# Making a part of the softmax exponentials as sums of fp16 bit patterns, with TensorE adding them up and GpSimd making one of them

## Chip, cores, metric

The kernel runs on one core of a Trainium2 chip. The metric is the device time of one execution in microseconds (us). Each kernel was run several times beside runs of the kernel before on the same chip. A run counts as "slow" when it is over 1.5% above the fastest run of the same kernel.

## The reference, cut to what matters

Two attention problems (32 heads of 16, 2048 positions) stand side by side. "A" works on four segments with a mask and a memory term. "B" is plain attention over all 2048 keys, and is most of the work:

```python
scores = jnp.einsum('bhqd,bhkd->bhqk', q, k) * Dh ** (-0.5)
p = _softmax(scores, axis=-1)
o = jnp.einsum('bhqk,bhkd->bhqd', p, v)
```

B has 4 query chunks x 4 row tiles x 2 = 32 units. A unit has 16 key blocks, and a key block has four banks of 128 keys x 512 queries (four heads), so 64 banks a unit. Each bank needs one exp of 128x512.

## The kernel before

ScalarE makes most of the exps, straight from PSUM, in tiles of alternately three and two banks. VectorE makes the exps of two of 16 key blocks of each unit but the first, by a polynomial on the bits of an fp16 number. TensorE makes scores (four 32-row matmuls can share the array), the products with V ("PV": four 32-column matmuls share it), the projections ("chores"), and fillers: matmuls on zeros, added into a live accumulator, whose only use is to keep TensorE's clock up. The order on each engine is fixed when the program is built.

```python
PESHARE = 0.74          # share of a tile's time that TensorE is to be filled to
VSHARE = 1.0            # dose of VectorE work a tile
VQUADS = 2              # key blocks of 16 that VectorE makes
PBUFS = 6
... # cut
        def idle_work(us):
            work[0] = min(max(work[0] - us * PESHARE, -1.0), 0.25)
            acc = accs.get(cur[0])
            while acc is not None and work[0] < -0.11:
                mm(acc[:], zeros[:, 0:P], zeros[:], start=False, stop=False, skip_group_check=True)
... # cut
        def vexp(q, xq):                 # xq: scores of one key block, scaled, as uint16 (128 x 2048)
            ... # cut
            ts(f[:].bitcast(U16), xq[:], 0x3FF, 0x3C00, ALU.bitwise_and, ALU.bitwise_or)
            tt(v[:], f[:], f[:], ALU.mult)
            ts(v[:], v[:], C3, C1 - 1.0, ALU.mult, ALU.add)
            tt(v[:], v[:], f[:], ALU.mult)
            ts(v[:], v[:], C0, 1024.0, ALU.add, ALU.mult)
            tt(xq[:].bitcast(I16), xq[:], v[:], ALU.add)
            ... # cut: handed to PV as one block
... # cut
        for t in range(NT):              # one tile of 3 or 2 banks
            run_until(t)
            scores(t)                    # TensorE scores, ScalarE exp
            did = pv(t - LAG, 2)         # up to two ready blocks
            ... # cut: chores
            idle_work(0.1 + 0.427 * len(tiles[t][0]))
            flush()
            vscores(t)                   # one bank of scores for VectorE, evicted as scaled uint16
            vfill(...)                   # pieces of VectorE work, as far as their dose goes
```

Scores for VectorE, PV accumulators and projections share three PSUM banks (`misc`). The ScalarE tiles have the other five.

## Time and profile before

| | before |
|---|---|
| time, median | 1050.2 us (of three runs; of the four of the result below, 1050.0) |
| ScalarE (ACT) busy | 984.7 of 1055.6 us |
| exps on ScalarE | 848 tiles, 973.5 us |
| filler matmuls | 1053 |
| mean granted TensorE clock | 0.976 |
| time at half clock | 52 us |

The first part of the page, busy time by engine:

```profile
span 1055.6 us, 17191 instructions
PE 967.6 (92%) x6822; PEld 277.2 (26%) x6822; DVE 759.8 (72%) x1108; ACT 984.7 (93%) x877; POOL 169.9 (16%) x335
```

Its second part, rows of 40 equal slices: busy tenths of PE and ACT, and the granted clock in tenths.

```profile
PE   8899999998999989999998999999999999999996
...
ACT  3799999998999989999999899999999999999995
...
PEclk8999999998999989999999899999999999999998
```

ACT is busy nearly throughout, apart from the start and the end. PE looks as busy, but a third of its matmuls' busy time are fillers, as the groups show (columns: line, engine, operation, out<-in, forms, count | busy us, mean ns | idle before, and what ended it):

```profile
L655 ACT ACTIVATE pT<-s_ps 128x1536 bf16<-128x1536 f32 x848 | 973.5, 1314 | 57.7 <-PE s_ps L80 53.0
...
L80 PE MATMUL acc<-zeros 128*128 128x512 bf16 x1053 | 321.6, 390 | 0.0
...
L596 DVE TENSOR_SCALAR vv<-vv 128x2048 f16<-128x2048 f16 x124 | 86.7, 699 | 2.2
L599 DVE TENSOR_TENSOR vv<-vf 128x2048 f16<-128x2048 f16 x62 | 76.2, 1229 | 1.9
```

The page also follows the chain of work that ended last back from the end, and gives each engine's share of it. ACT has the largest:

```profile
ACT 40%; PE 31%; issue 12%; DVE 11%; POOL 3%; DMA 1%; SPq 0%; ACTq 0%; DVEq 0%; POOLq 0%
```

The timeline at 299 us shows VectorE and GpSimd getting in each other's way (start, length, engine, what):

```profile
299.40 2.69 POOL L186 TENSOR_SCALAR qA<-qc,par 128x512 bf16<-128x512 bf16 x2 [18.40 <-DVE qc L183]
...
299.94 1.59 DVE L599 TENSOR_TENSOR vx<-vx,vv 128x2048 int16<-128x2048 uint16 x1
```

The VectorE operation takes 1.59 us instead of its usual 1.22, and the two GpSimd operations together 2.69 instead of about 1.4.

The waits: what ScalarE loses to TensorE, and what TensorE loses to VectorE's exps (total us, times, longest us).

```profile
ACT pT L655 <- PE s_ps L80: 53.0, 61, 8.0
...
PE acc L80 <- DVE vx L599: 3.9, 7, 1.0
...
PE v_ps L80 <- DVE vx L689: 0.7, 2, 0.5
```

### The profile page before, as it was taken

Reading aid. Unit: us, or ns where it says so; the run is one execution under the profiler, and the core shown is the slowest. Engines: PE = TensorE matmul, PEld = TensorE weight load, DVE = VectorE, ACT = ScalarE, POOL = GpSimd, SP = SyncE. Lnnn points to the kernel's source line nnn. Section 1 sums busy time; section 2 is a strip of 40 time slices with the busy share of each in tenths; the row PEclk is TensorE's granted clock in tenths of the full one; section 3 lists DMA queues with packets and bytes.
Section 4 is the critical chain, followed back from the end, with each engine's and each line's share of the span. In section 5 each row is a group of like instructions: output and inputs, shape, how many; then the busy total and the mean of one; then the engine's idle time right before and its main releaser. Section 6 shows DMA issues by size and latency. Waiting matters only on the chain.

```text
span 1055.6 us, 17191 instructions
## 1 busy us (share of the span) xinstructions
PE 967.6 (92%) x6822; PEld 277.2 (26%) x6822; DVE 759.8 (72%) x1108; ACT 984.7 (93%) x877; POOL 169.9 (16%) x335
## 2 busy tenths in 40 slices
PE   8899999998999989999998999999999999999996
PEld 2222222222222222222222222222222222222221
DVE  2668787866888677788876788858576787776654
ACT  3799999998999989999999899999999999999995
POOL 3721210403013030030302204021020300000000
PEclk8999999998999989999999899999999999999998
DMA  8400000001000000010000000000000000000000
GB/s 179 100 7 21 6 2 6 1 2 25 6 1 13 29 7 6 2 25 6 2 6 1 21 26 1 7 1 1 2 1 1 2 30 11 1 1 2 1 1 25
DMA packets 35642, 15.36 MB, mean 15 GB/s; under 512 B 27360, under 2 KB 35552, under 8 KB 35552
## 3 DMA queue, kind: packets, MB, share of 16 engines
q1 hardware_dynamic: 33776, 13.78, 5.5%
q8 instruction: 55, 0.90, 0.4%
q10 hardware_dynamic: 1776, 0.40, 0.2%
q14 instruction: 35, 0.29, 0.1%
HBM read 4.20 MB, written 4.19 MB: 8 GB/s over the span
## 4 chain that ended last, share of the span: by engine, by line
ACT 40%; PE 31%; issue 12%; DVE 11%; POOL 3%; DMA 1%; SPq 0%; ACTq 0%; DVEq 0%; POOLq 0%
ACT pT L655 39%; PE acc L80 14%; PE s_ps L80 8%; PE v_ps L80 5%; DVE vv L599 2%; DVE vx L689 2%; POOL pT L663 2%; PE q_ps L80 1%; PE k_ps L80 1%; DVE vx L599 1%; PE o_ps L80 1%; DVE vv L596 1%; ACT ex L194 1%; DVE vf L596 1%; DVE tT L253 1%
## 5 line engine op out<-in xcount | busy, mean ns | idle before, releaser
L655 ACT ACTIVATE pT<-s_ps 128x1536 bf16<-128x1536 f32 x848 | 973.5, 1314 | 57.7 <-PE s_ps L80 53.0
L80 PE MATMUL s_ps<-qB,KB 32*128 32x512 bf16 x1800 | 310.8, 384 | 35.0 <-ACT pT L655 30.5
L80 PE MATMUL acc<-zeros 128*128 128x512 bf16 x1053 | 321.6, 390 | 0.0
L689 DVE TENSOR_SCALAR vx<-v_ps 128x512 uint16<-128x512 f32 x248 | 169.1, 683 | 122.2 <-PE v_ps L80 65.7
L80 PEld LDWEIGHTS <-KB 32*128 32x128 bf16 x2048 | 99.6, 91 | 339.6 <-issue 326.7
L663 POOL TENSOR_SCALAR_AFFINE_SELECT pT<-pT 128x256 bf16<-128x256 bf16 (+2 forms) x242 | 111.0, 487 | 322.7 <-ACT pT L655 322.1
L80 PE MATMUL acc<-pT,VB 128*32 128x512 bf16 x1800 | 144.4, 385 | 1.2 <-DVE tT L253 1.2
L80 PEld LDWEIGHTS <-zeros 128*128 128x128 bf16 x1069 | 84.6, 99 | 147.2 <-issue 111.7
L253 DVE STREAM_TRANSPOSE tT<-acc 128x512 f32<-128x512 f32 x64 | 45.7, 714 | 94.1 <-PE acc L80 93.9
L80 PE MATMUL v_ps<-qB,KB 32*128 32x512 bf16 x248 | 95.5, 385 | 9.2 <-DVE aT L260 3.4
L596 DVE TENSOR_SCALAR vv<-vv 128x2048 f16<-128x2048 f16 x124 | 86.7, 699 | 2.2
L599 DVE TENSOR_TENSOR vv<-vf 128x2048 f16<-128x2048 f16 x62 | 76.2, 1229 | 1.9
L599 DVE TENSOR_TENSOR vx<-vx,vv 128x2048 int16<-128x2048 uint16 x62 | 76.0, 1226 | 1.2
L599 DVE TENSOR_TENSOR vv<-vv,vf 128x2048 f16<-128x2048 f16 x62 | 76.0, 1227 | 1.1
L80 PE MATMUL s_ps<-qA,kA 32*128 32x384 bf16 (+3 forms) x512 | 56.8, 313 | 9.9 <-ACT pT L655 7.8
L186 POOL TENSOR_SCALAR qB<-qc,par 128x512 bf16<-128x512 bf16 x32 | 26.0, 823 | 232.1 <-DVE qc L183 229.2
L80 PEld LDWEIGHTS <-VB 128*32 128x32 bf16 x2048 | 32.4, 94 | 73.9 <-issue 73.8
L596 DVE TENSOR_SCALAR vf<-vx 128x2048 uint16<-128x2048 uint16 x62 | 43.3, 699 | 1.5
L186 POOL TENSOR_SCALAR qA<-qc,par 128x512 bf16<-128x512 bf16 x32 | 25.7, 815 | 114.9 <-DVE qc L183 114.8
L80 PE MATMUL acc<-pT,vA 128*32 128x128 bf16 (+3 forms) x512 | 39.0, 332 | 5.6 <-POOL pT L663 3.2
L80 PEld LDWEIGHTS <-kA 32*128 32x128 bf16 x512 | 17.8, 92 | 63.1 <-issue 61.2
L80 PE MATMUL acc<-vx,VB 128*32 128x512 f16 x248 | 24.7, 386 | 4.6 <-DVE vx L599 3.9
(88 smaller groups left out, 510.8 us busy)
## 6 DMA issues: line engine op xcount, KB each, us to landing
out_dram<-osb SPq DMA_DIRECT2D x31, 128.0 KB, 1.7
w_b<-in_B_wqkv_dram SPq DMA_DIRECT2D x3, 512.0 KB, 6.0
phk<-phkT SPq DMA_TRANSPOSE x48, 2.3
w_a<-in_A_wv_dram SPq DMA_DIRECT2D x1, 512.0 KB, 7.0
wo_a<-in_A_wo_dram SPq DMA_DIRECT2D x1, 512.0 KB, 4.1
wo_b<-in_B_wo_dram SPq DMA_DIRECT2D x1, 512.0 KB, 5.0
w_a<-in_A_wk_dram SPq DMA_DIRECT2D x1, 384.0 KB, 7.5
w_a<-in_A_wq_dram SPq DMA_DIRECT2D x1, 384.0 KB, 8.2
```

What stands on the lines that cost most here:

```text
L80: return pin(nc.tensor.matmul(out, lhsT, rhs, **k))
L186: pin(nc.gpsimd.tensor_scalar(dst[:, e, :], qc[:], par[:, e:e + 1], 0.0, ALU.mult, ALU.add))
L194: pin(nc.scalar.activation(ex[:], src, ACT.Exp))
L253: vlater(0.72, lambda: pin(nc.vector.transpose(st["tT"][:, e].rearrange("p c d -> p (c d)"), acc)))
L596: pin(nc.vector.tensor_scalar(o, i, s1, s2, op0, op1))
L599: pin(nc.vector.tensor_tensor(o, i0, i1, op=op))
L655: pin(nc.scalar.activation(pT[:, 0:n, :], pt[:, 0:n, :], ACT.Exp, scale=SCALE))
L663: pin(nc.gpsimd.affine_select(out=blk, in_=blk, compare_op=ALU.is_ge, fill=0.0, base=0, pattern=[[0, len(sls)], [1, P]], channel_multiplie ...
L689: pin(nc.vector.tensor_scalar(x[0][:, vb[0], :], vt[:], XSCALE, 15360.0, ALU.mult, ALU.add))
```

## The change

The intent: take more exps off the bounding ScalarE. An fp16 bit pattern `x + offset` is a piecewise linear approximation of 2^x. Five such patterns at different offsets add up to a good exp, and the adding is free for VectorE, because TensorE sums them in PV. VectorE then needs four cheap adds a block instead of six operations, and one of the four is given to GpSimd. So VectorE can serve four and three key blocks of alternate units instead of two. A new `force()` makes sure that buffers are free: if the probabilities of six tiles ago are not yet used, it issues pending PV and VectorE pieces at once.

```diff
-C0, C1, C3 = 0.4580543, 0.4656991, 0.0762947
+LADDER = (12521, 12721, 12834, 13081, 13329)
-VQUADS = 2
+VBUFS = 9
+VQUADS = (4, 3)
+VPOOL = 1
...
-        def vexp(q, xq):            (six operations, shown above)
+        def vexp(q, buf, x):
+            for i, off in enumerate(LADDER[1:]):
+                yield 0.0 if i < VPOOL else 0.70
+                f = vtile()
+                if i < VPOOL:
+                    pin(nc.gpsimd.tensor_scalar(f[:], x[:], 1.0, float(off - LADDER[0]), ALU.mult, ALU.add))
+                else:
+                    pin(nc.vector.tensor_scalar(f[:], x[:], float(off - LADDER[0]), 32767.0, ALU.add, ALU.min))
+                vready(q, [1], f, 2 * (i < VPOOL))      # each pattern is one more PV block
+                vdone(buf)
...
         def scores(t):
+            while apend.get(t - PBUFS):
+                force()
...
+        def force():
+            if pv(NT, 1):
+                return
+            if vwork and vlive[0] < VBUFS:
+                vpiece(vwork)
+                return
+            assert step_chore()
... (cut: the plan of which tile gets which bank, separate weight tiles to free memory, bounds of the sums)
```

More of the change, by code (lines that the diff above doesn't have):

```diff
@@ L31 @@
 MASK_NEG = -1.0e9
-SUMS = {"a": (2.0 ** -8, 2.0 ** 31), "b": (2.0 ** 7, 2.0 ** 15.5)}
+SUMS = {"a": (2.0 ** -8, 2.0 ** 31), "b": (2.0 ** 9, 2.0 ** 15)}
 XSCALE = SCALE * 1.4426950408889634 * 1024
-C0, C1, C3 = 0.4580543, 0.4656991, 0.0762947
+LADDER = (12521, 12721, 12834, 13081, 13329)
 PESHARE = 0.74
@@ L41 @@
 VSHARE = 1.0
-VWAIT = 3
-VQUADS = 2
+VBUFS = 9
+VQUADS = (4, 3)
+VEND = 0.83
+VLEAD = 12
+VPOOL = 1
 BANKS = (3, 2)
@@ L135, in masks_gates, with load_w @@
         pin(nc.vector.scalar_tensor_tensor(grow[:], gv[:, :, 1], par[:, 1:2], grow[:], ALU.mult, ALU.add))
-    def load_w(pool, name):
-        t = pool.tile([P, 4, 3 * D], BF16, name=f"w_{name}", tag=f"w_{name}")
+    def load_w(homes, name):
+        t = [p.tile([P, 4, D], BF16, name=f"w_{name}", tag=tag, bufs=bufs) for p, tag, bufs in homes]
         srcs = ([B_wqkv[:, i * D:(i + 1) * D] for i in range(3)] if name == "b" else [A_wq, A_wk, A_wv])
         def load(eng, i, lo=0, hi=D):
-            eng.dma_start(out=t[:, :, i * D + lo:i * D + hi],
+            eng.dma_start(out=t[i][:, :, lo:hi],
                           in_=srcs[i][:, lo:hi].rearrange("(cc p) n -> p cc n", p=P))
@@ L169, in do_k @@
         for cc in range(4):
-            mm(ps[:], w[:, cc, D + rt * P:D + (rt + 1) * P], xT[:, cc, :], start=(cc == 0), stop=(cc == 3))
+            mm(ps[:], w[1][:, cc, rt * P:(rt + 1) * P], xT[:, cc, :], start=(cc == 0), stop=(cc == 3))
             if cc == 3:
@@ L178, in do_q @@
         for cc in range(4):
-            mm(ps[:], w[:, cc, rt * P:(rt + 1) * P], xT[:, cc, :], start=(cc == 0), stop=(cc == 3))
+            mm(ps[:], w[0][:, cc, rt * P:(rt + 1) * P], xT[:, cc, :], start=(cc == 0), stop=(cc == 3))
             if cc < 3:
@@ L204, in do_v @@
         for cc in range(4):
-            mm(ps[:], xT[:, cc, kb * P:(kb + 1) * P], w[:, cc, 2 * D:3 * D], start=(cc == 0), stop=(cc == 3))
+            mm(ps[:], xT[:, cc, kb * P:(kb + 1) * P], w[2][:, cc, :], start=(cc == 0), stop=(cc == 3))
             if cc == 3:
@@ L335 @@
         mp = ps_a = ms.enter_context(tc.tile_pool(name="ps_a", bufs=3, space=PSUM))
-        wA, ld = load_w(big, "a")
+        wA, ld = load_w([(big, f"wa{i}", 1) for i in range(3)], "a")
         ld(nc.scalar, 1, 0, P)
@@ L345 @@
         ld(nc.sync, 0, P)
-        wB, ld = load_w(big, "b")
+        wB, ld = load_w([(big, "wb0", 1)] + [(wk, "vx", VBUFS)] * 2, "b")
         ld(nc.sync, 1)
@@ L391 @@
                         quads_left[u["id"]] = quads_left.get(u["id"], 0) + 1
-                spans.append([(name, ch, rt), banks, []])
+                spans.append([(name, ch, rt), banks, None])
             else:
                 for u in us:
-                    quads_left[u["id"]] = S // P
-                    nv = VQUADS if nb else 0
-                    if nb:
-                        spans[-1][2].extend((u, kb) for kb in range(nv))
+                    nv = u["nv"] = VQUADS[nb % 2] if nb else 0
+                    quads_left[u["id"]] = S // P + nv * (len(LADDER) - 1)
@@ L400 @@
                     spans.append([(name, ch, rt) if u is u0 else None,
-                                  [(j, [(u, kb, 0, 512, 0)]) for kb in range(nv, S // P) for j in q4], []])
+                                  [(j, [(u, kb, 0, 512, 0)]) for kb in range(nv, S // P) for j in q4], u])
                     nb += 1
-        for i in range(1, len(spans)):
-            key = spans[i][0]
-            if key and key[0] == "a" and spans[i][2]:
-                spans[i - 1][1] += spans[i][1]
-                spans[i - 1][2] += spans[i][2]
-                spans[i - 1].append((key, len(spans[i - 1][1]) - len(spans[i][1])))
-                spans[i] = None
@@ L411 @@
-        first_tile, tiles = {}, []
-        vq = deque()
-        act = deque()
-        def close(n, v=None):
-            tiles.append(([act.popleft() for _ in range(n)], v))
-        for sp in spans:
-            if sp is None:
-                continue
-            starts = {0: sp[0]} if sp[0] else {}
-            for key, at in sp[3:]:
-                starts[at] = key
-            for u, kb in sp[2]:
-                vq.append((u, kb, set(q4)))
-            nv, na, placed = sum(len(left) for *_, left in vq), len(sp[1]), 0
-            for i, bank in enumerate(sp[1]):
-                if i in starts:
-                    first_tile[starts[i]] = len(tiles)
-                act.append(bank)
-                n = BANKS[len(tiles) % 2]
-                if len(act) < n:
-                    continue
-                v = None
-                if vq and placed < nv and (placed + 0.5) * na <= nv * (i + 1):
-                    js = vq[0][2] - {j for j, _ in act}
-                    if js:
-                        j = min(js)
-                        u, kb, left = vq[0]
-                        left.discard(j)
-                        if not left:
-                            vq.popleft()
-                        first_tile.setdefault(("v", u["ch"], u["rt"]), len(tiles))
-                        v = (j, (u, kb, 0, 512, 0))
-                        placed += 1
-                close(n, v)
@@ L446 @@
-        assert not vq
-        while act:
-            close(min(BANKS[len(tiles) % 2], len(act)))
+        first_tile, tiles, act, tile_of = {}, [], deque(), []
+        for key, banks, u in spans:
+            if key:
+                first_tile[key] = len(tiles)
+            if u:
+                u["lo"] = len(tile_of)
+            for bank in banks:
+                act.append(bank)
+                tile_of.append(len(tiles))
+                if len(act) == BANKS[len(tiles) % 2]:
+                    tiles.append([act.popleft() for _ in range(len(act))])
+            if u:
+                u["hi"] = len(tile_of)
@@ new lines, with plan @@
+        while act:
+            tiles.append([act.popleft() for _ in range(min(BANKS[len(tiles) % 2], len(act)))])
+        vplan = deque()
+        bs = [u for *_, u in spans if u]
+        def plan(u, kbs, lo, hi):
+            for i in range(4 * len(kbs)):
+                t = tile_of[int(lo - VLEAD + (i + 0.5) * (hi - lo) / (4 * len(kbs)))]
+                first_tile.setdefault(("v", u["ch"], u["rt"]), t)
+                vplan.append((t, u, kbs[i // 4]))
+        for u, nxt in zip(bs, bs[1:] + [None]):
+            n = max(u["nv"], 2)
+            cut = u["lo"] + (u["hi"] - u["lo"]) * ((n - 1) / n if nxt and nxt["lo"] == u["hi"] else VEND)
+            plan(u, range(1, u["nv"]), u["lo"], cut)
+            if nxt:
+                plan(nxt, range(1), cut, nxt["lo"])
@@ L520, in b_kv_chores, with counted @@
             v_ones(VB, S // P)
+            left = {"k": S // P, "v": S // P}
+            def counted(which, g):
+                yield from g
+                left[which] -= 1
+                vlive[0] -= left[which] == 0
             for rt in range(NRT):
@@ L524, in b_kv_chores @@
                     chore(min(d, first_tile.get(("v", 0, rt), NT)) if ch == 0 else d,
-                          do_k(mp, wB, xTB[ch], rt, KB[:, rt, ch * W:(ch + 1) * W]))
+                          counted("k", do_k(mp, wB, xTB[ch], rt, KB[:, rt, ch * W:(ch + 1) * W])))
             for sb in range(S // P):
                 chore(first_tile[("b", 0, 0)] + 4 + 4 * sb // 3,
-                      do_v(mp, wB, xTB[sb // 4], sb % 4, v_heads(VB, sb)[:, :, 0:DH]))
-        vfin, vwork, credit = deque(), deque(), [0.0]
+                      counted("v", do_v(mp, wB, xTB[sb // 4], sb % 4, v_heads(VB, sb)[:, :, 0:DH])))
+        vfin, vwork, credit, vlive = deque(), deque(), [0.0], [2]
         held[0] = []
@@ L577 @@
         last_s, cur = [None], [0]
-        pvq = []
+        pvq, forced = [], [0]
         accs, OT = {}, {}
@@ L589, in score, with vready, vdone, vtile @@
             mm(dst[:, col:col + w], k, q, start=first, stop=True, tile_position=(32 * j, 0), skip_group_check=True)
-        vx, live = {}, [0]
-        def vexp(q, xq):
-            def ts(o, i, s1, s2, op0, op1):
-                pin(nc.vector.tensor_scalar(o, i, s1, s2, op0, op1))
-            def tt(o, i0, i1, op):
-                pin(nc.vector.tensor_tensor(o, i0, i1, op=op))
-            yield 0.69
-            assert live[0] < 3
-            live[0] += 1
-            f = wk.tile([P, 4, 512], F16, name="vf", tag="vf")
-            v = wk.tile([P, 4, 512], F16, name="vv", tag="vv")
-            ts(f[:].bitcast(U16), xq[:], 0x3FF, 0x3C00, ALU.bitwise_and, ALU.bitwise_or)
-            yield 1.22
-            tt(v[:], f[:], f[:], ALU.mult)
-            yield 0.69
-            ts(v[:], v[:], C3, C1 - 1.0, ALU.mult, ALU.add)
-            yield 1.22
-            tt(v[:], v[:], f[:], ALU.mult)
-            yield 0.69
-            ts(v[:], v[:], C0, 1024.0, ALU.add, ALU.mult)
-            yield 1.22
-            tt(xq[:].bitcast(I16), xq[:], v[:], ALU.add)
-            pd = xq[:].bitcast(F16)
+        vx, apend = {}, {}
+        def vready(q, buf, x, late=0):
             u, kb = q
-            pvq.append(dict(u=u, kb=kb, t=now[0], v=True, parts=[(pd, j, j, (u, kb, 0, 512, 0)) for j in q4]))
+            pd = x[:].bitcast(F16)
+            pvq.append(dict(u=u, kb=kb, t=now[0] + late, v=buf, parts=[(pd, j, j, (u, kb, 0, 512, 0), None) for j in q4]))
             pvq.sort(key=lambda q: q["u"]["id"])
+        def vdone(buf):
+            buf[0] -= 1
+            vlive[0] -= buf[0] == 0
+        def vtile():
+            assert vlive[0] < VBUFS
+            vlive[0] += 1
+            return wk.tile([P, 4, 512], U16, name="vx", tag="vx", bufs=VBUFS)
+        def vexp(q, buf, x):
[8 more added lines that the diff above has]
+                vdone(buf)
         def vpiece(wq):
@@ L635, in vfill @@
                 wq = vfin or vwork
-                if wq is vwork and live[0] == 3 and not wq[0][2]:
+                if wq is vwork and vlive[0] == VBUFS:
                     return
@@ L646, in scores @@
         def scores(t):
-            banks, vb = tiles[t]
+            banks = tiles[t]
+            while apend.get(t - PBUFS):
+                force()
             pt = last_s[0] = ps_s.tile([P, BANKS[t % 2], 512], F32, name="s_ps", tag=f"s{t % 2}")
@@ L671, in scores @@
                         pvq.append(q)
-                    q["parts"].append((pT, sl, j, seg))
+                    q["parts"].append((pT, sl, j, seg, t))
                     q["t"] = t
+                    apend[t] = apend.get(t, 0) + 1
             pvq.sort(key=lambda q: q["u"]["id"])
         def vscores(t):
-            vb = tiles[t][1]
-            if vb is None:
-                return
-            vt = mp.tile([P, 512], F32, name="v_ps", tag="misc")
-            score(vt[:], vb[0], vb[1], True)
-            u, kb = vb[1][0:2]
-            if (u["id"], kb) not in vx:
-                while len(vwork) >= VWAIT:
-                    vpiece(vwork)
-                vx[u["id"], kb] = [wk.tile([P, 4, 512], U16, name="vx", tag="vx", bufs=VWAIT + 2), 0]
-            x = vx[u["id"], kb]
-            pin(nc.vector.tensor_scalar(x[0][:, vb[0], :], vt[:], XSCALE, 15360.0, ALU.mult, ALU.add))
-            x[1] += 1
-            if x[1] == 4:
-                vpush(vwork, vexp((u, kb), x[0]))
+            n = 0
+            while vplan and vplan[0][0] <= t and n < 1 + (vplan[0][0] < t - 3):
+                _, u, kb = vplan[0]
+                if (u["id"], kb) not in vx:
+                    if vlive[0] > VBUFS - 2:
+                        break
+                    vx[u["id"], kb] = [vtile(), set(q4)]
+                vplan.popleft()
+                x, left = vx[u["id"], kb]
+                j = min(left, key=lambda j: (j in {j for j, _ in tiles[t]}, j))
+                left.discard(j)
+                vt = mp.tile([P, 512], F32, name="v_ps", tag="misc")
+                score(vt[:], j, (u, kb, 0, 512, 0), True)
+                pin(nc.vector.tensor_scalar(x[:, j, :], vt[:], XSCALE, float(LADDER[0]), ALU.mult, ALU.add))
+                n += 1
+                if not left:
+                    buf = [len(LADDER)]
+                    vready((u, kb), buf, x)
+                    vpush(vwork, vexp((u, kb), buf, x))
+            return n
+        def force():
+            forced[0] += 1
+            if pv(NT, 1):
+                return
+            if vwork and vlive[0] < VBUFS:
+                vpiece(vwork)
+                return
+            assert step_chore()
         def unit_done(u):
@@ L739, in pv @@
                 pvq.remove(q)
-                live[0] -= "v" in q
+                if "v" in q:
+                    vdone(q["v"])
                 if u["id"] not in accs:
@@ L746, in pv @@
                 v = vA[u["ch"]] if u["name"] == "a" else VB
-                for pT, sl, j, (_, kb, col, w, c0) in q["parts"]:
+                for pT, sl, j, (_, kb, col, w, c0), at in q["parts"]:
+                    if at is not None:
+                        apend[at] -= 1
                     h = 8 * u["rt"] + 2 * j + u["e"]
@@ L770 @@
                 step_chore()
-            idle_work(0.1 + 0.427 * len(tiles[t][0]))
+            idle_work(0.1 + 0.427 * len(tiles[t]))
             flush()
-            vscores(t)
-            vfill((0.08 + 0.427 * len(tiles[t][0])) * VSHARE - (0.69 if tiles[t][1] else 0.0))
+            vfill((0.08 + 0.427 * len(tiles[t])) * VSHARE - 0.69 * vscores(t))
             flush()
@@ L779 @@
         flush()
-        vdrain(vwork)
+        assert not vplan
+        while vwork:
+            force()
         ot = OT[("b", NSEG - 1)]
@@ L841, in exact_problem @@
                 nc.gpsimd.memset(neg[32 * j:32 * j + 1, :], -1.0)
-            w, ld = load_w(big, name)
+            w, ld = load_w([(big, f"w{i}", 1) for i in range(3)], name)
             for i in (1, 0, 2):
```

## The prediction

> **What bounds the kernel now.** ScalarE. The page's first part gives ACT 984.7 of 1055.6 us, of which the exps `pT<-s_ps` are 973.5. By form: 424 tiles of three banks and 424 of two, so 0.459 us a bank of 512 columns. ACT idles 71 us: 24 in the first 50 us (busy by stretches), 53 behind PE's `s_ps` in all (the waits). PE shows 968 us busy, but 1053 of its matmuls are fillers on `zeros`, 0.216 us start to start in the timeline: 227 us. DVE 760 us (72%), POOL 170.
>
> **What the change does** (counted in the instruction order of both builds).
> - ACT: key blocks of B given to VectorE go from 62 to 108 (four banks each), s_ps banks of B from 1800 to 1616. ACT loses 184 x 0.459 = 84.5 us.
> - DVE: the polynomial goes: per block 3 x 0.70 + 3 x 1.23 = 5.8 us, x62 = 358 us. In come 184 more evictions `vx<-v_ps` (0.683), 126 us, and 324 adds on 128x2048, which I cost like `vf<-vx` (0.699), 226 us. DVE stays at about 755 us, in 7% less time.
> - PE: PV of VectorE blocks goes from 248 to 2160 matmuls. Four share the array (0.216 us a group; a change between row, column and full tiling costs 0.1 more, timeline), so +1728 net is +93 us. Fillers fall from 1053 to 387 (-144 us). My sum of groups and changes is 810 us after, 867 before: no new bound, though early stretches reach 93% of ACT's time.
> - POOL: 108 adds on 128x2048. `qA` and `qB` ops (512 columns) take 0.69 us undisturbed, masking shows 0.89 ns a column over 0.18 us; I estimate 2.2 us each, 240 us, POOL about 400.
>
> **The catch** is the shared port. The Trainium skill, "SBUF — State Buffer", section "Who interferes with whom", says that VectorE in a two-port mode, or with two SBUF inputs, and GpSimd lock each other out for a whole instruction. The trace agrees: at 300 us a `vx<-vx,vv` between two `qA` ops took 1.59 us instead of 1.22, the second `qA` 1.65 instead of 0.69. So far POOL's ops are short. The new one holds 2.2 us, and DVE's adds stand right after it. PSUM evictions don't collide. With a third of DVE's ops colliding, I estimate 1 us of DVE blocked per POOL add, some 110 us. Then DVE needs about 865 of 950 us; in the middle, where demand already is 54 of each 60 us of ACT, more than ACT's time. Late evictions hold the three `misc` banks, PE waits in order, scores come late, ACT idles.
>
> **On the critical path.** ACT's 84 us are nearly all on it (exp is 39% of the chain of waits; the rest mostly feeds it). I expect 15 to 25 us given back as ACT idle behind `s_ps`: 1050 - 84 + 19 = 985 us, range 950 to 1022. Faster by over 2%: 0.89; within 2%: 0.08; slower: 0.03.
>
> **What would show it.** `pT<-s_ps` at 889 us in 775 instructions, ACT still the busiest; ACT's idle behind `s_ps` 60 to 90 us; DVE `vx<-vx` 324 times with a mean of 0.9 to 1.1 us, not 0.70; POOL `vx<-vx` 108 times at 2 to 3 us; `acc<-zeros` 387; PE waiting longer for DVE's `vx<-v_ps`.
>
> **What would make it wrong.** A POOL add of 4 us or more, which would make DVE the bound (over 1000 us); lock waits that mostly fall in DVE's idle time (then 960); a lower granted clock with fewer fillers (now 0.98); sums outside the new bounds, which would run the exact path.

## The result

The changed kernel took 1192.9 us (median; 1177.6 to 1198.1) against 1050.0: slower, by a ratio of 1.124 (95% interval 1.113 to 1.135). Ratios are the mean time of one kernel's fast runs over that of the other's of the same rounds, so not quite the ratio of the medians.

| | before | after |
|---|---|---|
| profile's span | 1055.6 us | 1175.8 us |
| ACT busy / idle | 984.7 / 71 | 920.7 / 255 |
| mean clock | 0.976 | 0.868 |
| time at half clock (spells) | 52 us (8) | 313 us (28) |
| ACT idle at full clock / at half clock | 43 / 21 us | 75 / 173 us |
| PE's active area in full-clock windows | 0.58 | 0.49 |
| PE idle (span less busy, from the page) | 88 us | 170 us |
| PE's time lost to the half clock | 18 us | 115 us |

All rows from the fourth on, but PE's idle time, are worked out from the trace. The trace records the granted clock as stretches of 1.0 or 0.5 (the last one reaches some 2 us past the last instruction). Each idle gap of ACT over 50 ns was put down to the clock at its middle. "Active area" is, for a window of 3.41 us (the step in which those records change), the sum over its matmuls of columns at full clock times the share of the 128x128 array they use. A filler counts 1, four PV matmuls together 1, one bank of scores 0.25. For the last row each matmul's columns were laid out from its start (512 columns take 0.216 us at full clock and 0.427 us at half, from start to start of fillers in the trace) and overlaps merged; of what fell into half-clock stretches, the part that full clock would have saved is the time lost. The last two rows are good to some 10 us, because 119 of the changed kernel's 7884 matmuls have no record.

The same lines of the page as before:

```profile
span 1175.8 us, 19385 instructions
PE 1005.4 (86%) x7765; PEld 259.3 (22%) x7884; DVE 842.1 (72%) x1244; ACT 920.7 (78%) x804; POOL 387.6 (33%) x441
```

```profile
PE   7997897898879889789888988988898888889886
...
ACT  4798866889787578687889857857888788798985
...
PEclk8999958989797878897999887857879899898997
```

ACT has holes everywhere, mostly where the clock row drops. And it has lost its place in the chain that ended last:

```profile
PE 47%; DVE 25%; ACT 13%; issue 8%; POOL 3%; DMA 1%; SPq 1%; DVEq 0%; ACTq 0%; POOLq 0%
```

So TensorE, with VectorE before it, is the new bound. The groups:

```profile
L648 ACT ACTIVATE pT<-s_ps 128x1536 bf16<-128x1536 f32 (+1 forms) x775 | 908.4, 1256 | 242.0 <-PE s_ps L83 236.3
...
L606 POOL TENSOR_SCALAR vx<-vx 128x2048 uint16<-128x2048 uint16 x108 | 231.0, 2142 | 418.8 <-DVE vx L685 188.4
...
L608 DVE TENSOR_SCALAR vx<-vx 128x2048 uint16<-128x2048 uint16 x324 | 308.6, 990 | 1.7
...
L83 PE MATMUL acc<-zeros 128*128 128x512 bf16 x326 | 119.4, 431 | 6.7 <-issue 6.6
```

ScalarE's work fell (973.5 to 908.4 us), but its wait for scores rose from 53 to 236 us. The adds of VectorE take 0.99 us instead of 0.70, as foreseen. (Of the 387 fillers of the program the trace has 326. Some records are missing.)

```profile
ACT pT L648 <- PE s_ps L83: 236.3, 215, 10.5
...
PE acc L83 <- DVE vx L608: 30.9, 38, 1.9
PE v_ps L83 <- DVE vx L685: 21.7, 44, 2.0
...
PE acc L83 <- POOL vx L606: 12.6, 12, 2.0
```

These three are 65 us; all of TensorE's waits for VectorE and GpSimd in this view add up to 115 us, against 34 before. How such waits make a hole for ACT shows in one place, the timeline from 684 us:

```profile
682.81 1.45 ACT L648 ACTIVATE pT<-s_ps 128x1536 bf16<-128x1536 f32 x1 [0.99 <-PE s_ps L83]
...
684.21 2.44 POOL L606 TENSOR_SCALAR vx<-vx 128x2048 uint16<-128x2048 uint16 x1 [3.39 <-PE acc L83]
684.21 6.49 DVE L608 TENSOR_SCALAR vx<-vx 128x2048 uint16<-128x2048 uint16 x5
684.94 0.40 PE L83 MATMUL acc<-vx,VB 128*32 128x512 f16 x4 [0.83 <-DVE vx L608]
...
687.24 1.82 PE L83 MATMUL acc<-vx,VB 128*32 128x512 f16 x16 [1.90 <-DVE vx L608]
```

and the busy times in windows around it (window, length, busy us of PE, PEld, DVE, ACT, POOL, then the clock):

```profile
680.40:683.90 3.50, 2.87 (x26) 0.82 (x24) 3.05 (x5) 2.51 (x3) 0.41 (x1) 1.00 0.00 0
683.90:687.30 3.40, 0.66 (x12) 0.16 (x11) 3.40 (x4) 0.36 (x1) 2.44 (x1) 1.00 0.00 0
687.30:690.70 3.40, 1.76 (x16) 0.38 (x16) 3.39 (x3) 0.00 (x0) 2.10 (x1) 0.56 0.00 0
690.70:694.10 3.40, 3.35 (x28) 0.86 (x27) 2.58 (x4) 0.00 (x0) 1.25 (x1) 0.50 0.02 5
694.10:697.50 3.40, 3.15 (x31) 0.81 (x28) 1.42 (x3) 2.52 (x3) 2.52 (x2) 0.94 0.00 0
```

A GpSimd add of 2.44 us holds up VectorE's adds (five in a row take 6.49 us, at 0.70 they would take 3.5). PE waits 0.83 and 1.90 us for them and is busy 0.66 of 3.4 us. One window later the clock is halved, and ACT does nothing in the two windows from 687.3 to 694.1 us.

The same timeline over a wider window (679 to 698 us) shows the whole hole:

```profile
684.21 8.49 DVE L608 TENSOR_SCALAR vx<-vx 128x2048 uint16<-128x2048 uint16 x8
...
690.75 3.05 PE L83 MATMUL acc<-vx,VB 128*32 128x512 f16 x24 [1.69 <-DVE vx L608]
...
694.81 1.02 ACT L648 ACTIVATE pT<-s_ps 128x1024 bf16<-128x1024 f32 x1 [10.55 <-PE s_ps L83]
```

From 683.5 to 694.1 us TensorE issues PV only and no scores. It waits a third time, and ACT is idle for 10.55 us. The half clock explains little of this hole: VectorE's eight adds in a row, which show no wait for TensorE, last until 692.70, and scores start at 694.15, so at full clock they could have come some 0.7 us sooner (an estimate from these times). Yet the middle of the hole lies at half clock, and the row "ACT idle at half clock" counts all of it. That row says when ACT was idle, not why: a wait of TensorE starves ACT and also comes before a drop of the clock.

TensorE's own account is fairer. Its idle time rose by 82 us, and its time lost to the half clock by 96 us, while its matmuls took some 60 us less (fewer fillers). Together that is about the 120 us by which the span grew. It is an account of where the time went, and no proof of what caused it.

Over the whole trace, all 26 drops of the clock between the start and the end came after a window with an active area of at most 0.38, and the lowest area of a window that was followed by full clock was 0.29. In the kernel before, the five drops came at 0.35 or less. This is a correlation. The experiments test its parts.

### The profile page after: what moved, and what is told of

It reads as the page before. It is cut to its first block, busy times and chain, and to the rows that moved or that the text cites. A ratio compares the mean times of both kernels' runs of the same rounds, so it can differ in the third digit from the quotient of the medians.

```text
span 1175.8 us, 19385 instructions
## 1 busy us (share of the span) xinstructions
PE 1005.4 (86%) x7765; PEld 259.3 (22%) x7884; DVE 842.1 (72%) x1244; ACT 920.7 (78%) x804; POOL 387.6 (33%) x441
## 4 chain that ended last, share of the span: by engine, by line
PE 47%; DVE 25%; ACT 13%; issue 8%; POOL 3%; DMA 1%; SPq 1%; DVEq 0%; ACTq 0%; POOLq 0%
PE acc L83 21%; ACT pT L648 12%; DVE vx L608 11%; PE s_ps L83 11%; PE v_ps L83 10%; DVE vx L685 6%; PE o_ps L83 2%; PE k_ps L83 2%; POOL pT L656 1%; PE q_ps L83 1%; DVE tT L256 1%; POOL vx L606 1%; ACT ex L197 1%; DMA w_a<-in_A_wv_dram 1%; DVE tT L290 1%
## 5 line engine op out<-in xcount | busy, mean ns | idle before, releaser
L648 ACT ACTIVATE pT<-s_ps 128x1536 bf16<-128x1536 f32 (+1 forms) x775 | 908.4, 1256 | 242.0 <-PE s_ps L83 236.3
L685 DVE TENSOR_SCALAR vx<-v_ps 128x512 uint16<-128x512 f32 x432 | 293.0, 683 | 217.3 <-PE s_ps L83 167.2
L606 POOL TENSOR_SCALAR vx<-vx 128x2048 uint16<-128x2048 uint16 x108 | 231.0, 2142 | 418.8 <-DVE vx L685 188.4
L83 PE MATMUL s_ps<-qB,KB 32*128 32x512 bf16 x1616 | 352.3, 425 | 19.3 <-ACT pT L648 11.7
L608 DVE TENSOR_SCALAR vx<-vx 128x2048 uint16<-128x2048 uint16 x324 | 308.6, 990 | 1.7
L83 PE MATMUL acc<-vx,VB 128*32 128x512 f16 x2160 | 220.6, 443 | 51.4 <-DVE vx L608 30.9
L83 PE MATMUL v_ps<-qB,KB 32*128 32x512 bf16 x432 | 182.5, 422 | 45.3 <-DVE vx L685 21.1
L83 PE MATMUL acc<-zeros 128*128 128x512 bf16 x326 | 119.4, 431 | 6.7 <-issue 6.6
L83 PE MATMUL s_ps<-qA,kA 32*128 32x512 bf16 (+3 forms) x512 | 63.0, 310 | 5.9 <-ACT pT L648 4.1
L83 PEld LDWEIGHTS <-zeros 128*128 128x128 bf16 x403 | 34.0, 102 | 88.4 <-issue 80.8
```

The costliest lines, as they stand in the source:

```text
L83: return pin(nc.tensor.matmul(out, lhsT, rhs, **k))
L606: pin(nc.gpsimd.tensor_scalar(f[:], x[:], 1.0, float(off - LADDER[0]), ALU.mult, ALU.add))
L608: pin(nc.vector.tensor_scalar(f[:], x[:], float(off - LADDER[0]), 32767.0, ALU.add, ALU.min))
L648: pin(nc.scalar.activation(pT[:, 0:n, :], pt[:, 0:n, :], ACT.Exp, scale=SCALE))
L685: pin(nc.vector.tensor_scalar(x[:, j, :], vt[:], XSCALE, float(LADDER[0]), ALU.mult, ALU.add))
```

## The experiments

Theory A: the shared port makes VectorE late, TensorE waits for it in order, its activity falls, its clock is halved, and ScalarE starves. Rival B: there are simply too few fillers. Rival C: TensorE cannot carry the 1728 added PV matmuls even at full clock.

### e1_short: take the lock away, leave the rest

```diff
-pin(nc.gpsimd.tensor_scalar(f[:], x[:], 1.0, off, ...))
+pin(nc.gpsimd.tensor_scalar(f[:, 0, 0:64], x[:, 0, 0:64], 1.0, off, ...))
 # PV of this pattern reads f[:, 0, 0:64] eight times; orders of PE, DVE and ACT are the same
 # (off stands for float(off - LADDER[0]) here and below)
```

> The changed kernel with GpSimd's add cut from 2048 to 64 columns (the PV matmuls of this pattern read the 64 columns eight times, so PE's instructions are the same in order and size; the output is wrong on purpose). It takes away the lock of the shared port and leaves all else. Theory A (the lock makes VectorE late, PE waits for it in order, PE's activity in some 3.4 us windows falls too low and its clock is halved): DVE vx<-vx at 0.70 us instead of 0.99, time at half clock from 313 us to under 120 us, mean clock over 0.94, time 980 to 1040 us. Rival B (the plan simply has too few fillers for PE's clock, lock or no lock): clock stays under 0.90, time over 1130 us. Rival C (PE cannot carry the 1728 more PV matmuls even at full clock): clock may be high, but ACT still idles over 180 us behind s_ps at full clock, time over 1080 us.

1059.6 us (1051.7 to 1069.6), ratio to before 1.010 (1.003 to 1.017).

The clock row and the group of VectorE's adds:

```profile
PEclk8999967999996996999999999599999999999999
...
L608 DVE TENSOR_SCALAR vx<-vx 128x2048 uint16<-128x2048 uint16 x324 | 210.4, 689 | 1.7
```

VectorE's adds are at 0.69 us, the half-clock time falls from 313 to 112 us, and ACT's idle time at half clock from 173 to 45 us. At full clock it stays (75 to 87). So the long GpSimd add is worth about 133 us of time. On TensorE's account both terms fell: idle from 170 to 97 us, time lost to the half clock from 115 to 42. (The edit takes away more than the lock: TensorE's waits for GpSimd itself, its add and the masks behind it, fell from 24 to 7 us; those for VectorE from 91 to 52.) B is out as the main cause, because the fillers are the same 387. But 1060 is above my 980 to 1040: something else keeps back the rest. (The output passed the comparison although one pattern in five was wrong, so passing says little about the precision of such patterns.)

### e2_dve5: the same add on VectorE

```diff
-pin(nc.gpsimd.tensor_scalar(f[:], x[:], 1.0, off, ALU.mult, ALU.add))
+pin(nc.vector.tensor_scalar(f[:], x[:], off, 32767.0, ALU.add, ALU.min))
```

> The changed kernel with GpSimd's add given to VectorE at the same place in the program: PE and ACT have the same order. VectorE gets 108 more adds of 0.70 us (76 us) and no long GpSimd instruction. Theory A: the lock cost VectorE about 94 us by the trace (324 x 0.29), so VectorE's total is about the same but its longest single hold is 0.7 instead of 2.4 us; clock 0.90 to 0.96, time 1010 to 1100 us. If lateness of VectorE as such (its total), not the lock, is the cause: same time as the changed kernel, 1150 to 1200 us. Rival B: also about 1190 us.

1118.6 us, ratio 1.058; clock 0.887 in the profile. VectorE's 74 us of added work cost 59 us against e1_short, but less than GpSimd's add cost by its lock. VectorE's total therefore matters too, and GpSimd is the worse place for the add.

### e3_fill90: more fillers

```diff
-PESHARE = 0.74
+PESHARE = 0.90
```

> The changed kernel with fillers dosed for 0.90 of the time instead of 0.74: 939 instead of 387 filler matmuls. Theory A: the waits for VectorE and GpSimd stay, so some windows still fall below what keeps the clock, but cold spells end sooner; clock 0.90 to 0.95, time 1080 to 1150 us. Rival B: clock over 0.96, time 990 to 1040 us. Rival C: PE gets more work yet, time over 1200 us.

1189.2 us, the same as without. Yet the clock rose from 0.868 to 0.941 and the half-clock time fell from 313 to 142 us. ACT's idle at half clock fell from 173 to 104 us and rose at full clock from 75 to 140. The 552 added fillers (at 0.216 us 119 us) cost as much of PE's time as they won. My figure for theory A was missed. Part of C is true: PE has no time to spare.

### e4_lean: the kernel before with 387 fillers

```diff
-PESHARE = 0.74
+PESHARE = 0.57
```

> The kernel before, with fillers dosed for 0.57 of the time instead of 0.74: 387 filler matmuls as in the changed kernel, and no other change. Its area-weighted work falls lower than that of the changed kernel (no PV to replace the fillers), about 0.44 of PE's time. Theory A alone: few waits of PE, clock over 0.93, time 1055 to 1090 us. Rival B: clock under 0.88 and time over 1130 us. If it collapses, fillers are needed for the clock by themselves.

1164.9 us (1152.6 to 1174.5), clock 0.737, 610 us at half clock, active area 0.46. So with hardly an added wait (PE idle 107 us against 88), fewer fillers alone can bring the clock down and cost 114 us. Theory A alone had 1090 at most and is wrong there. The runs show two ways to lose the clock, fewer fillers here and waits in the changed kernel; both lower the active area.

### e5_split4: the GpSimd add in four pieces

```diff
-pin(nc.gpsimd.tensor_scalar(f[:], x[:], 1.0, off, ALU.mult, ALU.add))
+for j in q4:
+    pin(nc.gpsimd.tensor_scalar(f[:, j, :], x[:, j, :], 1.0, off, ALU.mult, ALU.add))
```

> The changed kernel with GpSimd's add of 2048 columns split into four of 512: the same work, nearly the same total hold of the port (four of about 0.6 us), but VectorE can get in between. PE's order is the same. Theory A (the length of one hold makes VectorE late at the wrong moment): longest vx<-vx on DVE falls from 2.4 to about 1.4 us, clock over 0.90, time 1090 to 1150 us. If only the total of the hold counts: vx<-vx stays at 0.95 to 1.0 us in the mean, time 1170 to 1200 us. Separate names for the two: length against total.

1142.6 us, ratio 1.082. VectorE's adds average 0.88 us, the longest is 1.14 us instead of 2.41. GpSimd's total even grew (338 us instead of 231). So splitting helps by some 50 us. Whether it is the length of one hold that matters is not shown, because VectorE's blocked time in all also fell: 324 x (0.879 - 0.689) = 62 us instead of 98.

### e6_locks: the lock alone, in the kernel before

```diff
+for _ in range(2 if q[0]["ch"] else 0):
+    pin(nc.gpsimd.tensor_scalar(xTB[0][:].bitcast(U16), xq[:], 1.0, 200.0, ALU.mult, ALU.add))
 f = wk.tile([P, 4, 512], F16, name="vf", tag="vf")
```

> The kernel before, with two GpSimd adds on 128x2048 added for each VectorE key block from the second chunk on (96 in all), from its vx tile into an input tile that is no longer read. Nothing reads the result, so no engine waits for the data; only the port is held, about 205 us. PE, ACT and DVE have the same instructions. Theory A: DVE's 16-bit operations on SBUF get longer by about 90 us in total, PE waits for DVE, the clock falls below 0.95, time 1090 to 1170 us. If the changed kernel's trouble is its PV matmuls or fillers and not the lock: under 1070 us.

1210.3 us (1196.1 to 1215.1), ratio 1.140 (1.127 to 1.153): beyond my range, and as slow as the changed kernel (1.113 to 1.135), if not slower. In the groups of its profile (of a slower run):

```profile
L604 POOL TENSOR_SCALAR xT_b<-vx 128x2048 uint16<-128x2048 uint16 x96 | 235.0, 2448 | 422.5 <-DVE vx L691 418.5
...
L599 DVE TENSOR_TENSOR vv<-vf 128x2048 f16<-128x2048 f16 x62 | 132.9, 2144 | 1.9
```

`vv<-vf`, which follows the GpSimd adds, goes from 1.23 to 2.14 us. Half-clock time goes from 52 to 259 us. No engine waits for the result of these 96 adds. So long GpSimd operations alone, with no more PV and with all 1053 fillers, bring a slowdown of this size about. The port is not their only way to do so. TensorE also waits for GpSimd's masks of A, which now stand behind the added operations in GpSimd's queue (3.2 us in the kernel before), as long as for VectorE's exps (3.9 before):

```profile
PE acc L80 <- DVE vx L599: 26.6, 13, 4.2
PE acc L80 <- POOL pT L665: 26.6, 10, 4.3
```

In all, its waits for VectorE rose from 28 to 92 us and those for GpSimd from 6 to 30, so the larger part comes through VectorE. No run separates the two.

### e7_q22: the new exp, with the old share

```diff
-VQUADS = (4, 3)
+VQUADS = (2, 2)
```

> The changed kernel with two of 16 key blocks a unit for VectorE instead of four and three: 62 blocks as in the kernel before, so ACT's work is as before, VectorE loses 224 us of work, GpSimd makes 62 adds, PE has 765 fillers. It tells the new way of making exp from the greater share. Theory A: VectorE has so much slack that the lock hardly matters: clock over 0.95, time 1040 to 1070 us. If the lock hurts whatever the slack: over 1090 us.

1096.4 us, ratio 1.040, although VectorE was busy only 632.6 us. Slack on VectorE does not make the long GpSimd add harmless. Here also PE waited 20 us for GpSimd's masking of A tiles, which stands behind its adds (3 us in the kernel before).

### e8_three: three patterns, all on VectorE

```diff
-LADDER = (12521, 12721, 12834, 13081, 13329)
+LADDER = (13337, 13618, 14003)
-VPOOL = 1
+VPOOL = 0
```

> The changed kernel with three patterns instead of five, all made by VectorE (own least-squares offsets: sum within 0.8% of exp against 0.24% with five, by arithmetic), so no long GpSimd instruction, 108 x 2 adds on VectorE, 1296 PV matmuls of VectorE blocks instead of 2160, 532 fillers. It takes away the lock and most of the added PV and VectorE work, but keeps ACT's gain of 84 us. By the arithmetic of the prediction 970 to 1000 us if the lock, lateness and PE's load are all that stood in the way; clock over 0.96. If ACT's time itself was misjudged: over 1020 us.

994.1 us (982.7 to 1015.5), ratio 0.933 (0.923 to 0.943), correct. The clock row and the exps of the profiled run (a slower one, 998.6 us):

```profile
PEclk8999999999995799977999999999999999999999
...
L648 ACT ACTIVATE pT<-s_ps 128x1536 bf16<-128x1536 f32 (+1 forms) x775 | 895.2, 1294 | 76.7 <-PE s_ps L83 71.1
```

ACT's gain was real, and most of it (56 us in the medians, of the 84 predicted) arrives once lock, adds and PV shrink. This version beats both kernels. It was the fastest of all that ran.

### e9_pv3 and e10_pv5: PV or adds?

Both have no long GpSimd operation, and wrong outputs on purpose.

```diff
 # e9: 324 adds as in the changed kernel, only 3 of 5 patterns go to PV (1296 matmuls)
 # e10: 3 patterns (216 adds), two of them given to PV twice (2160 matmuls)
```

> No long GpSimd instruction; VectorE makes the changed kernel's 324 adds a run, but TensorE sums only three of the five patterns (the first is not made, one is made and not used; output wrong on purpose): 1296 PV matmuls of VectorE blocks, 553 fillers, as with three patterns. With the run without the lock (324 adds, 2160 matmuls: 1060 us) and the three patterns (216 adds, 1296 matmuls: 983 us in its fast runs) this is a corner of a square. If PE's added PV is what is left once the lock is gone: 980 to 1005 us. If VectorE's load is: 1040 to 1065 us.

> The other corner: three patterns made by VectorE (216 adds), two of them summed twice by TensorE, so 2160 PV matmuls and 369 fillers as in the changed kernel (output wrong on purpose), no long GpSimd instruction. If PE's added PV is what is left: 1040 to 1065 us, clock 0.93 to 0.95. If VectorE's load is: 980 to 1005 us.

e9: 1040.1 us (1030.9 to 1052.8), ratio 0.988. e10: 1025.1 us, but from 1000.3 to 1049.9 with clocks of 0.991 to 0.925, one fast run only. Both lie between the other two corners (994 and 1060), so both loads seem to count. For PV this rests on e10's one fast run (1000.3 us, against 983 to 989 for e8's), and the fillers differ too (553 and 369). How the loads divide stays open, because e10 scatters as much as the difference.

### e11_fill80 and e12_two: fillers and fewer patterns

```diff
 # e11: e8_three with PESHARE = 0.80 (750 fillers for 532)
 # e12: LADDER = (14004, 14508), VPOOL = 0, VQUADS = (5, 4)
```

> Three patterns by VectorE, with fillers dosed for 0.80 instead of 0.74 (750 instead of 532). The profile of three patterns still had 85 us at half clock. If the clock is worth more than PE's time here: 970 to 980 us, clock over 0.985; if PE's time is short by now: 990 to 1010 us at a better clock.

> Two patterns by VectorE (sum within 1.5% of exp by arithmetic) and five and four of 16 key blocks a unit: ACT loses another 31 blocks, 57 us, VectorE gets 139 adds of 2048 columns and 556 evictions, 1112 PV matmuls of VectorE blocks, 456 fillers. If ACT still bounds: 930 to 960 us. If PE or VectorE take over: 970 to 1000 us.

e11: 1001.4 us, ratio 0.952, clock 0.984 in its fast profile. No gain over e8, which reached 983 at clock 0.980. e12: 1045.1 us, from 997.5 to 1107.2 with clocks of 0.935 to 0.820. ACT had 860.5 us to do, the least so far, and gained nothing: a miss, and the clock is what varies.

### e13_short12 and e14_share12: bursts in the program's order?

By then I suspected the new `force()`. In the built program of the changed kernel it issues 134 steps at 16 tiles, up to 23 in a row, and none of them makes scores. A dose of 1.2 brings it to 19 steps. (The hole at 684 us looks like such a stretch: PV and adds, and no scores.)

```diff
 # e13: e1_short with VSHARE = 1.2;  e14: the changed kernel with VSHARE = 1.2 (349 fillers each)
-VSHARE = 1.0
+VSHARE = 1.2
```

> The version without the lock (GpSimd's add on 64 columns), with VectorE's work dosed at 1.2 instead of 1.0 a tile, so that 19 steps are forced instead of 134. If the bursts are what is left: 985 to 1025 us, ACT's longest wait for s_ps under 5 us outside of start and end. If the load of VectorE and PE is: 1045 to 1070 us.

> The changed kernel with the dose at 1.2: the lock stays, the bursts mostly go. If the lock's cost comes mostly through bursts (adds in a row behind a GpSimd add while ScalarE waits): 1080 to 1140 us. If it comes everywhere alike: 1160 to 1195 us.

e13: 1036.4 us, ratio 0.987; ACT's longest wait for scores fell from 8.0 to 2.8 us. e14: 1223.9 us, ratio 1.161, clock 0.80, 494 us at half clock: worse, against the expectation of both readings. Without the lock the larger dose wins some 23 us. With it TensorE's idle time fell too, from 170 to 130 us, but its time lost to the half clock rose from 115 to 199 us. With fewer waits the run was still longer, so waits alone do not explain its time. The dose also leaves 349 fillers instead of 387, so neither run tests the bursts alone, and what part bursts have in the lock's 133 us stays open.

### e15_three12 and e16_two12: the same for three and two patterns

```diff
 # e15: e8_three with VSHARE = 1.2;  e16: e12_two with VSHARE = 1.2
```

> Three patterns by VectorE with the dose at 1.2: forced steps 21 to 4. If bursts matter: 965 to 985 us and fewer spells at half clock. If not: 983 to 995 us as before.

> Two patterns, five and four blocks a unit, with the dose at 1.2: forced steps 68 to 3. If bursts matter: 940 to 980 us and less scatter between runs. If VectorE's or PE's load is the limit: 1000 to 1060 us.

e15: 1038.6 us (1004.5 to 1059.3). e16: 1070.1 us (1041.8 to 1086.1). Both have a lower clock (0.898 and 0.835 in the profile). e15 is worse than e8 also in its one fast run (1004.5 us against 983 to 989), with the same number of fillers, so fewer bursts did not help there. For e16 the ranges overlap (e12: 997.5 to 1107.2), and it has 31 fillers less. The windows of e16's profile (of one of its slower runs; columns as above) show something else:

```profile
519.00:529.00 10.00, 10.00 (x55) 2.07 (x54) 6.08 (x11) 7.18 (x6) 4.61 (x13) 0.50 0.12 26
529.00:539.00 10.00, 10.00 (x57) 1.65 (x57) 6.27 (x12) 5.85 (x5) 1.66 (x4) 0.50 0.12 26
...
589.00:599.00 10.00, 10.00 (x45) 1.69 (x44) 2.59 (x7) 6.72 (x6) 1.37 (x2) 0.50 0.04 9
```

PE is busy all the time and stays at half clock for 89 us. One short lull comes before it (PE busy 1.75 of 3.40 us at 512.3). Then, at half speed, its mix of partly filled matmuls keeps an active area of 0.29 to 0.38, and the clock does not come back.

### e17_short_fill and e18_two_fill: give these two more fillers

```diff
 # e17: e13_short12 with PESHARE = 0.80 (527 fillers);  e18: e16_two12 with PESHARE = 0.82 (682)
```

> No lock, few bursts, five patterns' work, with fillers dosed for 0.80 (527 instead of 349). If the clock is what is left: clock over 0.97, time 995 to 1020 us. If PE's time is: clock up, but time within 1% of 1036 us or above.

> Two patterns, five and four blocks a unit, few bursts, with fillers dosed for 0.82 (682 instead of 425). If the clock is what is left: clock over 0.96, time 950 to 985 us, far less than 1070. If PE's time is: over 1030 us.

e17: 1027.2 us, ratio 0.977, clock 0.973 in the profile. The clock is nearly repaired and the time fell by 1%. I take it that PE's time is what remains (argued, not tested): by my sum of groups and changes of tiling, 848 us of issue (an estimate), with 61 us of waits at full clock on top. e18: 1024.5 us (1003.2 to 1041.7), 46 us better than e16, with a clock of 0.91 to 0.96 against 0.82 to 0.87: there more fillers and a better clock did help, but the run did not reach the 950 to 985 I expected.

## Why the prediction was wrong

- **Right: the work of each engine.** Exps at 775 instructions; 908 us busy against 889 predicted. GpSimd's add 2.14 us (2.2 estimated), VectorE's adds 0.99 us in the mean (0.9 to 1.1 predicted), so 324 x (0.990 - 0.689) = 98 us blocked (110 predicted). 387 fillers in the program.
- **Right: the way it starts.** VectorE late, TensorE waits in order, scores late, ACT idle. e1_short and e6_locks show that the long GpSimd operation starts it: taking it away wins 133 us, adding such operations to the kernel before loses 158. Most of TensorE's added waits are for VectorE, as the lock has it; a smaller part is for GpSimd itself.
- **Wrong: the step "no new bound" for PE, and with it "I expect 15 to 25 us given back as ACT idle behind `s_ps`".** ACT's wait behind `s_ps` rose by 183 us (53 to 236). The prediction had PE 810 us full, of some 935, and so left it room to wait. That sum holds at full clock and without waits. In the run PE's idle time, mostly waits, grew by 82 us (88 to 170), and the half clock cost it 96 us more (18 to 115; 512 columns take 0.427 us there, not 0.216). The chain that ended last went from ACT 40%, PE 31%, DVE 11% to PE 47%, DVE 25%, ACT 13%: PE and VectorE are the bound. The clock had no term in the sum at all, and the waits had one that was too small. How much of the 236 us each made is not shown. ACT's idle time rose by 32 us at full clock and by 152 us at half clock, but this split counts holes like that at 684 us as clock.
- **Wrong in kind: "a lower granted clock with fewer fillers".** I named it as a risk, but as a matter of the number of fillers. e4_lean shows that fewer fillers alone can do it. In the changed kernel it was chiefly the waits for the long GpSimd add and what it delays: with the same 387 fillers, e1_short has a clock of 0.947 and the changed kernel 0.868. And fillers are no remedy where PE is full (e3_fill90: clock up by 0.073, time the same).
- **What it rested on.** The fillers of the kernel are dosed by planned time, so that the plan has about the same active area as before (my arithmetic from the instruction counts, an estimate: 0.58 in both, if the changed kernel ran 935 us). The plan has no allowance for waits. Over 1176 us the same matmuls come to 0.46 (0.58 x 935 / 1176).
- **Open.** How the 60 to 75 us between e1_short and e8_three divide between VectorE's adds and PV; how much of the lock's 133 us comes by TensorE's waits and how much by its clock; and why a larger dose of VectorE work helped without the lock (e13) and hurt with it (e14) and with three patterns (e15).

## What to carry to other kernels

Where TensorE feeds the bounding engine, cost a change at both clocks, and count what it waits for in its program order before calling it "no new bound". Look up how near a typical 3.4 us window is to the activity at which the clock was last seen to drop (here 0.38), and expect a new wait to cost twice: in this kernel 0.83 and 1.90 us of waits in one such window came before a halved clock. Do not give GpSimd a long SBUF operation beside VectorE's two-port or two-input operations (as the Trainium skill, "SBUF — State Buffer", section "Who interferes with whom", names them) to "use an idle engine". Here 2 us of it a block cost more than doing it on VectorE (1193 against 1119 us). Before adding more hands, look for less work: three patterns instead of five, without GpSimd, made the same idea 6.7% faster instead of 12.4% slower.

## What the Trainium skill lacked or had wrong

- "TensorE: Matmul & The Clock Gate", section "What's actually happening": it says that the clock rises after at least one busy window of about 3.4 us, and that the gate follows how busy PE has been. The window agrees (records change in steps of 3.41 us). But in e16_two12 PE was busy 10.00 of 10.00 us in window after window and stayed at 0.50 for 89 us, with an active area of 0.29 to 0.38. (The ends of matmuls are modelled; by starts and columns it streamed some 0.85 of the time.) For getting the clock back, a measure weighted by the array's area fits better than busy time: over all 20 traces, 255 half-clock windows that were followed by full clock had a mean area of 0.38 and the 840 others 0.32, while both were busy (0.98 and 0.95). For losing it both measures do about as well. Only traces were compared for this, no experiment varied the area alone.
- The same page: it gives no level of activity. Here the clock dropped after windows with an area of 0.38 or less (26 of 26 in the changed kernel, 5 of 5 before); but six such windows of the changed kernel were followed by full clock, so it is no sharp threshold.
- "SBUF — State Buffer", section "Who interferes with whom": the lock is as described, and the hold is visible (0.69 to 2.41 us for one VectorE add). It lacks what the lock costs downstream: 98 us of VectorE time blocked went with 133 us of run time (e1_short).
- "SBUF — State Buffer", its summary of rules, advises to schedule whichever of the two is off the critical path. Splitting GpSimd's add into four also helped (longest VectorE add 2.41 to 1.14 us, time 1193 to 1143 us), which it does not mention.
